# Converting the weights in 32 pieces among the attention's steps instead of 16 calls between them

## The chip, the core and the metric

The kernel runs on one core of one Trainium2 chip. The metric is the device time of one execution in microseconds (us). The core's engines are TensorE (PE: matrix products and transposes, with PEld for its weight loads), VectorE (DVE), ScalarE (ACT), GpSimd (POOL) and SyncE (SP), which issues most DMA transfers. Each engine works through its own queue of instructions in order, and semaphores tie the queues together.

## What is computed

Two blocks follow one another. The first is attention in which a query sees only keys of its own cluster; the second is a feed-forward block (ffn) with an unusual gate.

```
B, H, S, D = 4, 8, 768, 64;  16 clusters
q_assign = argmax(q_n . c_n), k_assign = argmax(k_n . c_n)      # normalised
scores   = q k^T / sqrt(D), -1e9 where q_assign != k_assign
attn     = softmax(scores);  y = attn v                         # (B, H, S, D)
x        = y as (B*S, H*D) = (3072, 512)
h        = x w_in                                               # w_in  512 x 2048
g        = h * erf(softplus(h))
out      = g w_out                                              # w_out 2048 x 512
```

The weights w_in and w_out arrive as 64-bit floats, of which the kernel sees pairs of 32-bit words (low word, high word). It makes 32-bit floats of them by integer and float operations on the words: a shift of the high word, a mask that turns numbers too small into zero, the low word scaled by the number's power of two and added, and the sign put back. Everything else is 32-bit float, with some tiles in bf16.

## The kernel before

**Attention.** The 32 pairs (batch, head) are worked off two heads at a time, as 16 "pairs" p; four of them (HP) make a batch. For each pair `route(p)` (L212) transposes q and k on TensorE (tile `pt`), ScalarE copies them out of PSUM (L228, L230), and GpSimd casts them to bf16 into the lower half of `qm` and `km` (L232). Then come the similarities to the centroids (`psim`, `sims`), their maxima on VectorE (`mx` L257, L259, `mr` L267 with GpSimd's product L263 between them), the one-hot codes `aq` and `ak` (L269), and their transposes `pb` (L282), copied into `qm` and `km` (L290, L292). `shift(p)` (L297) makes 12 tiles `sm` of masked maxima and reduces each on VectorE (`nmx`, L308); the result `nm` (L313) goes through DRAM (`line`, L322 and L325) into one row of `qm`.

`scores(u)` (L338) works on one of a pair's 12 units (half of the queries, one of NJ = 6 key blocks): four products into `sc` (L345, L351), ScalarE's exponential into `pr` (L356) and GpSimd's running sum `acc` (L360, L364). `attend(u0)` (L368) makes the products with v for a half (`av`, L375) and the sums (`psum`, L382); VectorE adds a constant (L386), takes the reciprocal (L387) and writes the ffn's input `xT` in three chunks (L396).

**The ffn.** There are 12 chunks of 256 tokens, three to a batch. `hidden(n)` (L424) makes `hp` (L432), copied to `g` (L439); `gate(n)` (L408) runs softplus and erf on ScalarE over the tile `a_s` in two halves each (L415) and multiplies on VectorE (L417); `project(n)` (L446) makes `po` (L451), `osb` and the output transfer.

**The order.** The program issues `route(0)` and `shift(0)`, then two units at a time. After each two units come five slots; in each slot `pump` (L482) issues ffn products up to an allowance of TensorE cycles (`per_slot`) and one step of the next pair's `route` and `shift` (`aside`, L492) is issued. A batch's ffn starts when its four pairs have been attended, so the first four pairs run without ffn, and the last batch's ffn stands alone at the end. The framework's scheduler then orders the instructions of each engine by the order of issue and by when their data and buffers are ready in its own plan; the order on an engine is fixed before the run.

**The conversion.** `convert` (L130) is called 16 times, for 128 x 1024 weights each: after two of every three double units of the first four pairs. Each call loads 1 MB into `raw64` through GpSimd's queue (L132), squares the high words on ScalarE (L138), and has seven operations on VectorE (L139, L144, L148, L151, L154, L157, L158) on the tiles `w_m` and `w_x`. The pools for raw words and scratch are closed when the fourth pair is nearly done, and the pools for `a_s`, `g` and `osb` are opened in their place (L515 to L519).

Of the kernel before, what the change touches and what calls it, by code (L numbers as in the profile page):

```python
# [17 lines left out]
P = 128  # L18
# [9 lines left out]
GW = 2  # L28
TB = 256
NCHUNK = B * S // TB  # L30
LC = 1024
TINY_HI = 2.0**-15 * 1.125
BIG = 2.0**60
# [4 lines left out]
XBUFS = (5, 6, 6)  # L38
# [4 lines left out]
def kernel(  # L43
# [22 lines left out]
    xTp = pool("xTp", 1)  # L66
    linep = pool("linep", 2, space=bass.MemoryType.DRAM)
# [37 lines left out]
    wpool = ExitStack()  # L105
    setup = wpool.enter_context(tc.tile_pool(name="setup", bufs=1))
# [20 lines left out]
    wraw = wpool.enter_context(tc.tile_pool(name="wraw", bufs=2))  # L127
    wtmp = wpool.enter_context(tc.tile_pool(name="wtmp", bufs=2))

    def convert(dst, src):  # L130
        raw = wraw.tile([P, LC, 2], U32, name="raw64")
        nc.gpsimd.dma_start(out=raw.rearrange("p (a n) w -> p a (n w)", a=src.shape[1]), in_=src)  # L132
        hi, lo = raw[:, :, 1], raw[:, :, 0]
        m = wtmp.tile([P, LC], U32, name="w_m")
        x = wtmp.tile([P, LC], U32, name="w_x")
        mf, xf = m.bitcast(F32), x.bitcast(F32)

        nc.scalar.activation(out=xf, in_=raw.bitcast(F32)[:, :, 1], func=ACT.Square)  # L138
        nc.vector.tensor_scalar(  # L139
            out=x.bitcast(I32), in0=xf, scalar1=TINY_HI**2, scalar2=-1.0,  # L140
            op0=ALU.is_ge, op1=ALU.mult,
        )

        nc.vector.tensor_scalar(  # L144
            out=m, in0=hi, scalar1=3, scalar2=0x7FFFFFFF,
            op0=ALU.logical_shift_left, op1=ALU.bitwise_and,
        )
        nc.vector.scalar_tensor_tensor(  # L148
            out=m, in0=m, scalar=0x40000000, in1=x, op0=ALU.bitwise_xor, op1=ALU.bitwise_and
        )  # L150
        nc.vector.tensor_scalar(  # L151
            out=x, in0=m, scalar1=0x7F800000, scalar2=None, op0=ALU.bitwise_and
        )
        nc.vector.scalar_tensor_tensor(  # L154
            out=xf, in0=lo, scalar=2.0**-52, in1=xf, op0=ALU.mult, op1=ALU.mult
        )
        nc.vector.tensor_tensor(out=xf, in0=mf, in1=xf, op=ALU.add)  # L157
        nc.vector.scalar_tensor_tensor(  # L158
            out=dst.bitcast(U32), in0=hi, scalar=0x80000000, in1=x,
            op0=ALU.bitwise_and, op1=ALU.bitwise_or,  # L160
        )

    w_steps = []
    for c in range(0, DFF, LC):
        for r in range(DM // P):
            rows = moe_w_in[r * P : (r + 1) * P, 2 * c : 2 * (c + LC)]
            w_steps.append((w_in[:, r, c : c + LC], rows.unsqueeze(1)))
    n = LC // DM
    for f in range(0, NFT, n):
        rows = moe_w_out[f * P : (f + n) * P].rearrange("(t p) m -> p t m", p=P)  # L170
        w_steps.append((w_out[:, f : f + n].rearrange("p t m -> p (t m)"), rows))
# [3 lines left out]
    sq = setup.tile([P, D], F32, name="sq")  # L175
# [20 lines left out]
    cn = setup.tile([P, 2, D], F32, name="cn")  # L196
# [15 lines left out]
    def route(p):  # L212
        st = pairs[p]
        for nm in "qk":
# [3 lines left out]
            for half in range(2):  # L218
# [6 lines left out]
                dst = raw[:, half * HW : (half + 1) * HW]  # L225
                src = pt.rearrange("p j t -> p (j t)")
                if nm == "q":
                    nc.scalar.mul(out=dst, in_=src, mul=D**-0.5)  # L228
                else:
                    nc.scalar.copy(out=dst, in_=src)  # L230
                for e in range(2):
                    nc.gpsimd.tensor_copy(  # L232
                        out=low[(1 - e) * D : (2 - e) * D, e, half * HW : (half + 1) * HW],
                        in_=raw[e * D : (e + 1) * D, half * HW : (half + 1) * HW],
                    )
# [32 lines left out]
        for i, (dst, op) in enumerate(((aq, ALU.is_equal), (ak, ALU.not_equal))):  # L268
# [7 lines left out]
            )  # L276
        yield
# [90 lines left out]
    def attend(u0):  # L368
# [17 lines left out]
        nc.vector.tensor_scalar_add(out=den, in0=psum, scalar1=S * EPS)  # L386
# [21 lines left out]
    def gate(n):  # L408

        h = gs[n]  # L410
        s = late_pools["act"].tile([P, NFT, TB], F32, name="a_s")
        half = NFT // 2
        for func, src in ((ACT.Softplus, h), (ACT.Erf, s)):
            for i in range(0, NFT, half):
                nc.scalar.activation(out=s[:, i : i + half], in_=src[:, i : i + half], func=func)  # L415
        for i in range(0, NFT, GW):
            nc.vector.tensor_tensor(  # L417
                out=h[:, i : i + GW], in0=s[:, i : i + GW], in1=h[:, i : i + GW], op=ALU.mult
            )

    gs = {}
    late_pools = {}

    def hidden(n):  # L424
        b, c = n // CPB, n % CPB
        gs[n] = late_pools["g"].tile([P, NFT, TB], F32, name="g")
        for fp in range(NFT // GW):
            hp = ps_f.tile([P, GW, TB], F32, name="hp", tag="f")
# [17 lines left out]
    def project(n):  # L446
        b, c = n // CPB, n % CPB
        for tt in range(TJ):
            po = ps_f.tile([P, DM], F32, name="po", tag="f")
            for ft in range(NFT):  # L450
                nc.tensor.matmul(  # L451
# [5 lines left out]
            osb = late_pools["out"].tile([P, DM], F32, name="osb")  # L457
# [5 lines left out]
    def ffn_stream():  # L463

        late = iter(())
        for n in range(NCHUNK):
            while (n // CPB + 1) * HP > len(xTs):
                yield None
            for i, cost in enumerate(hidden(n)):
                yield cost  # L470
                if i >= 2 * GW * HP:
                    for _ in range(2):
                        if (x := next(late, None)) is not None:
                            yield x
# [83 lines left out]
```

## Time and profile before

| | |
|---|---|
| median of 3 runs | 1337.95 us (1336.57 to 1338.3) |
| the profiled execution, its own time | 1337.45 us |
| its span, first to last instruction | 1335.5 us |
| PE busy | 1218.0 us (91%) |
| DVE busy | 640.5 us (48%) |
| ACT busy | 421.0 us (32%) |
| POOL busy | 400.2 us (30%) |
| mean granted TensorE clock | 0.966 |

The busy time of an engine is the time in which at least one of its instructions ran; the time in which it only waited or set registers is not counted. In the rows of a group, "x16 | 27.5, 1718 | 0.3" means 16 instructions, 27.5 us busy together, 1718 ns the mean of one, and 0.3 us in which the engine stood idle just before them. In a timeline row the first number is the start in us, the second the length in us, and square brackets tell how long the engine had been idle and what released it. In a table of stretches each row is one part of the span; the columns are the length, each engine's busy time with its instructions in brackets, the granted TensorE clock, the share in which the DMA engines were busy, and the rate. A row of waits has the total, how often, and the longest, in us.

### The profile page before, as it was taken

The numbers are of one execution on the slowest core, as the hardware profiler recorded it, in microseconds if no ns is written. First come the engines' busy times: TensorE is split into PE (matmuls) and PEld (weight loads), VectorE is DVE, ScalarE is ACT, GpSimd is POOL, SyncE is SP. The second block draws the span as 40 slices with busy tenths as digits, with TensorE's granted clock in tenths as the row PEclk, the third lists the DMA queues.
The fourth block names the chain that finished last, engine by engine and source line by source line (L and its number), as shares of the span: only waits on it lengthen the run. The fifth ranks groups of instructions, "written<-read, shape, count | busy, mean of one in ns | idle before, by whom it ended". The sixth has DMA issues, their size and how long they took to land.

```text
span 1335.5 us, 13090 instructions
## 1 busy us (share of the span) xinstructions
PE 1218.0 (91%) x5313; PEld 659.5 (49%) x5313; DVE 640.5 (48%) x809; ACT 421.0 (32%) x458; POOL 400.2 (30%) x337
## 2 busy tenths in 40 slices
PE   3676767889999999999999999999999999999998
PEld 1222222346546545444654645545645646575764
DVE  6898999746243525451634534452615413221221
ACT  3232323224416224414423422514424413130321
POOL 3536365452323233423233231522232221000000
PEclk9777889899999999999999999999999999999999
DMA  6213142110101001101001010102000000000000
GB/s 166 87 64 120 42 130 75 24 37 1 36 8 32 12 13 40 36 1 40 12 1 51 2 44 8 36 1 52 1 9 20 1 8 9 8 9 8 8 16 16
DMA packets 82699, 42.90 MB, mean 32 GB/s; under 512 B 76464, under 2 KB 76496, under 8 KB 81616
## 3 DMA queue, kind: packets, MB, share of 16 engines
q1 hardware_dynamic: 79312, 25.31, 7.7%
q0 software_dynamic: 3328, 16.78, 3.7%
q8 instruction: 41, 0.67, 0.2%
q14 instruction: 18, 0.15, 0.0%
HBM read 35.73 MB, written 6.34 MB: 32 GB/s over the span
## 4 chain that ended last, share of the span: by engine, by line
PE 72%; DVE 16%; POOL 4%; ACT 3%; DMA 2%; issue 2%; SPq 0%; POOLq 0%; ACTq 0%; DVEq 0%
PE po L451 24%; PE hp L432 21%; PE av L375 8%; PE sc L345 7%; PE sm L304 4%; DVE nmx L308 3%; DVE den L387 2%; POOL acc L364 2%; PE psum L382 2%; ACT pr L356 2%; PE sc L351 2%; DVE w_x L154 2%; PE pt L221 1%; DVE w_x L157 1%; DVE w_m L148 1%
## 5 line engine op out<-in xcount | busy, mean ns | idle before, releaser
L432 PE MATMUL hp<-xT,w_in 128*128 128x256 f32 x1536 | 379.6, 384 | 0.0
L451 PE MATMUL po<-w_out,g 128*128 128x512 f32 x768 | 370.4, 599 | 2.6 <-DVE g L439 2.0
L364 POOL TENSOR_TENSOR acc<-acc,pr 128x768 f32<-128x768 f32 x128 | 224.2, 1751 | 489.8 <-ACT pr L356 483.0
L432 PEld LDWEIGHTS hp<-xT,w_in 128*128 128x128 f32 x1536 | 284.8, 191 | 99.2 <-issue 67.0
L356 ACT ACTIVATE pr<-sc 128x768 f32<-128x768 f32 x192 | 152.5, 812 | 386.7 <-PE sc L351 384.5
L308 DVE TENSOR_REDUCE nmx<-sm 128x2 f32<-128x768 f32 x192 | 178.6, 953 | 110.0 <-PE sm L304 108.7
L439 DVE COPY g<-hp 128x512 f32<-128x512 f32 x96 | 66.0, 688 | 286.8 <-PE hp L432 286.6
L345 PE MATMUL sc<-qT,kT 64*128 64x384 f32 x768 | 187.1, 549 | 10.3 <-DVE nmx L308 8.4
L451 PEld LDWEIGHTS po<-w_out,g 128*128 128x128 f32 x768 | 139.4, 190 | 107.4 <-issue 90.6
L375 PE MATMUL av<-pr,in_v 128*64 128x386 f32 x768 | 160.1, 511 | 6.6 <-DVE xT L396 6.2
L304 PE MATMUL sm<-km,qm 128*128 128x384 bf16 x384 | 99.1, 347 | 25.8 <-DVE nmx L308 13.7
L345 PEld LDWEIGHTS sc<-qT,kT 64*128 64x128 f32 x768 | 69.2, 199 | 92.5 <-issue 42.1
L360 POOL TENSOR_TENSOR acc<-pr,pr 128x768 f32<-128x768 f32 x32 | 60.6, 1894 | 152.8 <-ACT pr L356 152.6
L375 PEld LDWEIGHTS av<-pr,in_v 128*64 128x64 f32 x768 | 54.8, 139 | 85.4 <-issue 74.8
L415 ACT ACT_TABLE_LOAD x48 | 61.6, 1283 | 105.3 <-DVE g L439 104.5
L417 DVE TENSOR_TENSOR g<-a_s,g 128x512 f32<-128x512 f32 x96 | 66.2, 740 | 50.5 <-ACT a_s L415 50.5
L386 DVE TENSOR_SCALAR den<-psum 128x384 f32<-128x384 f32 x32 | 17.8, 556 | 147.9 <-PE psum L382 147.7
L304 PEld LDWEIGHTS <-qm 128*128 128x128 bf16 x384 | 36.3, 100 | 98.7 <-issue 84.2
L387 DVE RECIPROCAL den<-den 128x384 f32<-128x384 f32 x32 | 81.6, 2550 | 0.7
L351 PE MATMUL sc<-qm,km 64*128 64x384 bf16 x384 | 70.8, 339 | 0.2 <-DMA qm<-line 0.2
L415 ACT ACTIVATE a_s<-g 128x2048 f32<-128x2048 f32 x24 | 45.9, 1911 | 78.4 <-DVE g L439 78.3
L292 ACT COPY km<-pb 64x768 bf16<-64x768 bf16 x32 | 25.4, 793 | 117.8 <-PE pb L282 117.4
(76 smaller groups left out, 720.9 us busy)
## 6 DMA issues: line engine op xcount, KB each, us to landing
raw<-in_moe_w_in_dram POOLq DMA_DIRECT2D x8, 1024.0 KB, 5.7
raw<-in_moe_w_out_dram POOLq DMA_DIRECT2D x8, 1024.0 KB, 5.3
in_q<-in_q_dram SPq DMA_DIRECT2D x32, 192.0 KB
in_k<-in_k_dram SPq DMA_DIRECT2D x32, 192.0 KB
in_v<-in_v_dram SPq DMA_DIRECT2D x32, 192.0 KB
out_dram<-osb SPq DMA_DIRECT2D x24, 256.0 KB
qm<-line SPq DMA_DIRECT2D x32, 1.5 KB
line<-nmT SPq DMA_DIRECT2D x16, 3.0 KB
```

Of the source, the lines that this page charges most:

```text
L304: nc.tensor.matmul(sm[:, e, 0:HW], lhsT=st["qm"][:, e, t * P : (t + 1) * P], rhs=st["km"][:, e, half * HW : (half + 1) * HW], start=True, ...
L308: nc.vector.tensor_reduce(out=nmx[:, t, half], in_=sm[:, :, 0:HW], axis=AX.X, op=ALU.max, negate=True)
L345: nc.tensor.matmul(sc[:, e, 0:HW], lhsT=st["kT"][r, j * P : (j + 1) * P], rhs=st["qT"][r, cols], start=True, stop=False,)
L351: nc.tensor.matmul(sc[:, e, 0:HW], lhsT=st["km"][r, e, j * P : (j + 1) * P], rhs=st["qm"][r, e, cols], start=False, stop=True,)
L356: nc.scalar.activation(out=pr[:, :, 0:HW], in_=sc[:, :, 0:HW], func=ACT.Exp)
L364: nc.gpsimd.tensor_tensor(out=st["acc", half], in0=st["acc", half], in1=pr[:, :, 0:HW], op=ALU.add)
L375: nc.tensor.matmul(av[e * D : (e + 1) * D], lhsT=st["v"][:, j, e], rhs=prs[(u0 + j) % NPT][:, e], start=(j == 0), stop=(j == NJ - 1),)
L387: nc.vector.reciprocal(out=den, in_=den)
L415: nc.scalar.activation(out=s[:, i : i + half], in_=src[:, i : i + half], func=func)
L417: nc.vector.tensor_tensor(out=h[:, i : i + GW], in0=s[:, i : i + GW], in1=h[:, i : i + GW], op=ALU.mult)
L432: nc.tensor.matmul(hp[:, a], lhsT=w_in[:, r, f0 : f0 + P], rhs=xTs[b * HP + r][c], start=(r == 0), stop=(r == HP - 1),)
L451: nc.tensor.matmul(po, lhsT=gs[n][:, ft, tt * P : (tt + 1) * P], rhs=w_out[:, ft], start=(ft == 0), stop=(ft == NFT - 1),)
```

## The change

The conversion becomes a generator of three steps a piece, on 128 x 512 weights, 32 pieces. `prepare` draws steps from it: 1.5 for each step of `aside(0)`, 0.4 a slot in the first four pairs, and one a slot after that. The mask is made by ScalarE's Sign in place of L139, the addition L157 goes to GpSimd, and the raw words and the scratch lie in halves of the gate's tile `a_s`, which is now two buffers of half the size. Raw words are loaded through SP's queue, one piece ahead. All pools are open from the start; `hidden` and `project` are held back while the weights they need aren't issued. In `route`, ScalarE writes the bf16 copies directly from PSUM (three reads of each `pt`), and there is one more empty step ahead of `pb`. In `attend`, ScalarE adds the constant. `attend` for a finished half is issued right after the next half's first two units instead of ahead of the second two. `pump` keeps what it owes, up to 8 slots' worth, and issues at most twice the allowance at once. The second of the three xT chunks has 5 buffers instead of 6.

```diff
-LC = 1024
+LC = 512
+TINY_SQ = TINY_HI**2 * (1 - 2.0**-23)
-XBUFS = (5, 6, 6)
+XBUFS = (5, 5, 6)
...
+    actp = pool("actp", 2)
+    gp = pool("gp", 2)
+    outp = pool("outp", 2)
+    setup = pool("setup", 1)
...
+    def half_tile():
+        return actp.tile([P, NFT // 2, TB], F32, name="a_s")
+
+    def convert():
+        def fetch(n):
+            t = half_tile().rearrange("p f t -> p (f t)").bitcast(U32)
+            nc.sync.dma_start(out=t[:, 0 : 2 * LC], in_=w_steps[n][1])
+            raw = t[:, 0 : 2 * LC].rearrange("p (n w) -> p n w", w=2)
+            return raw, t[:, 2 * LC : 3 * LC], t[:, 3 * LC : 4 * LC]
+
+        def finish(n, raw, x):
+            nc.vector.scalar_tensor_tensor(
+                out=w_steps[n][0].bitcast(U32), in0=raw[:, :, 1], scalar=0x80000000, in1=x,
+                op0=ALU.bitwise_and, op1=ALU.bitwise_or,
+            )
+            converted[0] = n + 1
+
+        nxt, last = fetch(0), None
+        for n in range(len(w_steps)):
+            raw, m, x = nxt
+            hi, lo = raw[:, :, 1], raw[:, :, 0]
+            mf, xf = m.bitcast(F32), x.bitcast(F32)
+            nc.scalar.activation(out=xf, in_=hi.bitcast(F32), func=ACT.Square)
+            nc.scalar.activation(out=x.bitcast(I32), in_=xf, func=ACT.Sign, scale=-1.0, bias=tiny)
+            nc.vector.tensor_scalar(
+                out=m, in0=hi, scalar1=3, scalar2=0x7FFFFFFF,
+                op0=ALU.logical_shift_left, op1=ALU.bitwise_and,
+            )
+            if last:
+                finish(*last)
+            if n + 1 < len(w_steps):
+                nxt = fetch(n + 1)
+            yield
+            nc.vector.scalar_tensor_tensor(
+                out=m, in0=m, scalar=0x40000000, in1=x, op0=ALU.bitwise_xor, op1=ALU.bitwise_and
+            )
+            yield
+            nc.vector.tensor_scalar(
+                out=x, in0=m, scalar1=0x7F800000, scalar2=None, op0=ALU.bitwise_and
+            )
+            nc.vector.scalar_tensor_tensor(
+                out=xf, in0=lo, scalar=2.0**-52, in1=xf, op0=ALU.mult, op1=ALU.mult
+            )
+            nc.gpsimd.tensor_tensor(out=xf, in0=mf, in1=xf, op=ALU.add)
+            last = n, raw, x
+            yield
+        finish(*last)
...
-                dst = raw[:, half * HW : (half + 1) * HW]
-                if nm == "q":
-                    nc.scalar.mul(out=dst, in_=src, mul=D**-0.5)
-                else:
-                    nc.scalar.copy(out=dst, in_=src)
-                for e in range(2):
-                    nc.gpsimd.tensor_copy(
-                        out=low[(1 - e) * D : (2 - e) * D, e, half * HW : (half + 1) * HW],
-                        in_=raw[e * D : (e + 1) * D, half * HW : (half + 1) * HW],
-                    )
+                own = [(slice(e * D, (e + 1) * D), low[(1 - e) * D : (2 - e) * D, e, cols]) for e in range(2)]
+                for r, dst in [(slice(0, P), raw[:, cols])] + own:
+                    if nm == "q":
+                        nc.scalar.mul(out=dst, in_=src[r], mul=D**-0.5)
+                    else:
+                        nc.scalar.copy(out=dst, in_=src[r])
...
+        yield
         yield
...
-        nc.vector.tensor_scalar_add(out=den, in0=psum, scalar1=S * EPS)
+        nc.scalar.activation(out=den, in_=psum, func=ACT.Identity, bias=alleps)
...
+            while converted[0] < DM // P * ((fp + 1) * GW * P // LC):
+                yield None
...
+                while converted[0] < DM // P * (DFF // LC) + ft + 1:
+                    yield None
...
     def pump(cycles):
         owed[0] += cycles
-        while owed[0] > 0:
+        left = 2 * cycles
+        while owed[0] > 0 and left > 0:
             cost = next(stream, None)
             if cost is None:
-                owed[0] = 0
-                return
+                break
             owed[0] -= cost
+            left -= cost
+        owed[0] = min(owed[0], 8 * cycles)
...
+    def prepare(tenths):
+        due[0] += tenths
+        while due[0] >= 10:
+            due[0] -= 10
+            next(conv, None)
+
     for _ in aside(0):
-        pass
+        prepare(15)
...
-        if j == 2 and u >= NJ:
-            attend(u - 2 - NJ)
         scores(u)
         scores(u + 1)
-        if p < HP and j != 2 and w_steps:
-            convert(*w_steps.pop(0))
-        if (p, half, j) == (HP - 1, 1, NJ - 2):
-            wpool.close()
-            late_pools.update(act=pool("actp", 1), g=pool("gp", 2), out=pool("outp", 2))
+        if j == 0 and u:
+            attend(u - NJ)
         for _ in range(SLOTS):
-            pump(per_slot)
+            if len(xTs) >= HP:
+                pump(per_slot)
+            prepare(4 if p < HP else 10)
             next(ahead, None)
```

In the new file the piece's instructions stand at L167 (Square), L168 (Sign), L169, L178, L183, L186 (VectorE), L189 (GpSimd's addition) and L155 (`finish`).

## The prediction

> **What bounds the kernel now.** I read the page's slices first, then a table of busy time by stretch, then the groups of one line by shape, then VectorE (DVE) in order of time.
>
> ```profile
> span 1335.5 us, 13090 instructions
> PE   3676767889999999999999999999999999999998
> DVE  6898999746243525451634534452615413221221
> PEclk9777889899999999999999999999999999999999
> ```
>
> From the ninth slice TensorE is at 9 tenths and at full clock: there the time is TensorE's work. In the first eight slices (33.4 us each) TensorE stands at 3 to 8 and DVE at 9. I cut the span where each `shift` ends (the one row of `nm`, L313: 40.75, 93.7, 158.9, 217.4, 274.0):
>
> ```profile
> core 0: us, PE busy (x) PEld busy (x) DVE busy (x) ACT busy (x) POOL busy (x), PEclk, DMA share, GB/s
> 0.00:40.75 40.75, 19.40 (x66) 8.07 (x68) 28.45 (x65) 10.07 (x13) 10.34 (x29) 1.00 0.52 136
> 40.75:93.70 52.95, 33.93 (x138) 12.29 (x136) 48.26 (x50) 15.01 (x20) 24.10 (x19) 0.69 0.30 95
> 93.70:158.90 65.20, 43.80 (x194) 16.51 (x192) 59.73 (x59) 17.81 (x24) 31.67 (x23) 0.84 0.26 83
> 158.90:217.40 58.50, 44.05 (x196) 16.44 (x194) 55.97 (x57) 17.81 (x24) 33.57 (x23) 0.88 0.32 92
> 217.40:274.00 56.60, 41.95 (x198) 16.22 (x196) 47.33 (x47) 14.68 (x21) 30.12 (x20) 0.89 0.14 40
> ```
>
> Four pairs of heads take 53 to 65 us each and DVE is busy for 84 to 96% of that. After 274.0 TensorE is busy 1034.90 of 1061.50 us. So the change can win only in the first 274 us, in TensorE's 26.6 idle us after them, or by putting TensorE's later work earlier. What fills DVE there is the conversion, 16 calls of seven operations:
>
> ```profile
> L154 DVE SCALAR_TENSOR_TENSOR w_x<-raw,w_x 128x1024 f32<-128x1024 uint32 x16 | 27.5, 1718 | 0.3
> L157 DVE TENSOR_TENSOR w_x<-w_m,w_x 128x1024 f32<-128x1024 f32 x16 | 25.0, 1560 | 0.2
> L148 DVE SCALAR_TENSOR_TENSOR w_m<-w_m,w_x 128x1024 uint32<-128x1024 uint32 x16 | 23.9, 1491 | 0.3
> L151 DVE TENSOR_SCALAR w_x<-w_m 128x1024 uint32<-128x1024 uint32 x16 | 16.8, 1048 | 0.3
> L139 DVE TENSOR_SCALAR w_x<-w_x 128x1024 int32<-128x1024 f32 x16 | 14.8, 927 | 8.5 <-ACT w_x L138 8.4
> L144 DVE TENSOR_SCALAR w_m<-raw 128x1024 uint32<-128x1024 uint32 x16 | 14.4, 898 | 6.3 <-DMA raw<-in_moe_w_in_dram 6.3
> ```
>
> With L158 (24.6 us) that is 147 of the 240 us that DVE is busy before 274. The means are above the shortest instances (1.21 us for the four operations with two inputs or two steps on them, 0.68 for the three plain ones): 16 x (4 x 1.21 + 3 x 0.68) = 110, so 37 us are stretch. In time it looks so:
>
> ```profile
> 94.93 0.69 DVE L139 TENSOR_SCALAR w_x<-w_x 128x1024 int32<-128x1024 f32 x1
> 95.54 2.17 DVE L151 TENSOR_SCALAR w_x<-w_m 128x1024 uint32<-128x1024 uint32 x1
> 97.63 2.17 DVE L144 TENSOR_SCALAR w_m<-raw 128x1024 uint32<-128x1024 uint32 x1
> 99.72 2.70 DVE L154 SCALAR_TENSOR_TENSOR w_x<-raw,w_x 128x1024 f32<-128x1024 uint32 x1
> ```
>
> While POOL runs `acc` additions without a gap (three in 6.10 us from 95.24), every such DVE operation takes 1.48 us more, the 0.69 one as the 1.21 one.
>
> **The change on DVE.** Seven operations on 1024 elements become five on 512, 32 times. From the shapes of L396 (0.48 us for 256, 0.34 for 128: 1.06 ns an element) a 512 form costs 1.21 - 0.54 = 0.67, and the plain form at half that slope 0.41. A piece: 3 x 0.67 + 2 x 0.41 = 2.8; 32 pieces 91 us. The stretch is not known. Low: POOL's casts go as well (42.9 us of its work) and its instructions are no more than before, so a little under the 37 stays, 34, and DVE needs 125 (3.9 a piece). High: only POOL's long operations cause it, 41 `acc` and 5 products with `rank`, 0.8 us each, and the 32 new additions do the same: 37 + 26 = 63, so 154 (4.8 a piece). I take 3.9, because in 274 us POOL's busy time hardly changes: 129.8 - 42.9 + 32 x 1.2 (1.68 us for 768 elements in L364, with a fixed part) = 125. Both ends stay for the range.
>
> The Trainium skill, "SBUF — State Buffer", section "Who interferes with whom", speaks against small pieces: DVE with two inputs in SBUF, or in its two-port mode, and a GpSimd operation that reads SBUF exclude one another for a whole instruction. The 2.17 beside 0.69 agrees. By that rule the loss is per meeting, not per element, and the sum would be nearer to 154 than to 125.
>
> DVE busy before the fifth `shift` ends: 240 - 147 - 7 x 0.55 (L386 goes to ScalarE) + 125 = 214 us. It was idle 34. That alone would put the end at 248; but the new order adds waits, so I go by stretch. The built program's order on each engine shows that all 32 pieces stand on DVE ahead of the fifth `route`, none beside the ffn: 7 before the first `nm`, then about 7, 8, 8 and 2.
>
> **The waits it adds.** Square waits for its load on ScalarE; behind it stand exps, and TensorE's scores wait for those (ScalarE already idles 58.7 us at L138 for loads, and TensorE at most 4.2 us for ScalarE's exps there). L155 waits on DVE for POOL's addition, which may stand behind an `acc`; behind it stand reductions that free the score banks. The order puts the next piece's L169 or a reduction between, so from nothing to 32 x 1.2 = 38 us; nearest is `mr` waiting for POOL's product, 2.9 us in all: I take 0.2 us a piece, within the stretches below.
>
> **Start to first `nm`, 40.75 now: 57.** On ScalarE, Square and Sign of piece 0 stand before the first copy of `qT` (now at 7.34). They wait for a load queued on SP behind q and k; the first raw tile now lands at 10.36, so `qT` comes at about 11.5: +4. Each transposed half is now read by ScalarE three times (0.49 + 2 x 0.48); half of that hides behind `in_k`, for which TensorE waits 2.49 us now: +2. Two pieces stand before the first `mx`: the first `nmx` at 34 instead of 28.6. Between the twelve `nmx` (11.06 us without gaps now) stand four pieces, 11.6 us: 34 + 23 = 57.
>
> **Second stretch, 53 now: 50.** `nm` to `mx` 16: the mask line's way through DRAM (6 us from `nm` to L351, as at 274.0 to 280.1), then ScalarE in order: two exps, low copies, Square and Sign of two pieces, `sims`. `mx` to `nmx` 11 (9.3 now where nothing else is there, 246.60 to 255.92, and two pieces in its gaps). `nmx` to `nm`: twelve reductions 11.4, reciprocal and `xT` 3.3, two pieces 8: 23.
>
> **Third and fourth, 65.2 and 58.5 now: 55 each.** The order gives TensorE, between `nm` and `psim`, 10 score products (0.46), 11 mask products (0.17), 15 `av` (0.43), transposes and sums (3.7): 16.6 us at full clock, 20 at the 0.84 to 0.88 granted here, and 2 to `mx`: 22. Then 11 and 22. DVE's sum is 8 x 3.9 + 21.2 = 52, just below. **Fifth, 56.6 now: 49**: 22, 9.3 and 18 (255.92 to 273.96), as the rows of this stretch without conversion.
>
> 57 + 50 + 55 + 55 + 49 = 266: 8 us earlier than 274.
>
> **After that.** The remaining 1061.5 us are TensorE's. By the built order one score, five `av` and three hidden products fewer are left at the fifth `nm`: 0.5 + 2.1 + 1.5 = -4. Between halves of a transpose TensorE has some 1.4 us of other work, ScalarE needs 1.45: half of 33 gaps lose 0.25 us, +4 (without this cover of three hidden products it would be 1 us a gap, +33). 10 of the 26.6 idle us lie at 504 to 556, 634 to 660 and 920 to 946, where the next batch's attention runs with little ffn; the order gives these pairs about twice the ffn products (the pairs ahead of them fewer): -4. The wait of L282 for `aq` stays (same products ahead of it):
>
> ```profile
> PE pb L282 <- DVE aq L269: 13.3, 10, 2.4
> ```
>
> XBUFS of 5 holds one `av` back until a chunk's hidden products are done; TensorE has those meanwhile: 0. `gate` by halves does the same four activations: 0. ScalarE gets some 5 us a pair (345.6 busy of 1061.5): off the path. No table load stands at Square, Sign or Identity in the order. SP gets 32 loads of 512 KB between q, k and line transfers; a piece asks two ahead, 4 us (1 MB lands in 5.5), inside the 6 to 7 us of a piece.
>
> Sum: 1335.5 - 8 - 4 = 1323.5; the profiled run was 1337.45 for that span (+1.95), and the median of the runs 1337.95, 0.5 above it. **Forecast 1325 us**, own range 1315 to 1333.
>
> **Rivals.**
> - *DVE's sum is the bound* (chance 0.22). For: DVE is 84 to 96% busy now. Against: the chain `nm` to `mx`. The fifth `nm` at 248: 26 + 4 earlier, 1307.
> - *The order eats it* (0.14): pieces at the start cost 16 to 18 us, the pairs give back just as much (52 + 57 + 57 + 51 after 58): 275, 1334 to 1337. For: TensorE's 22 us ahead of `mx` in every pair. That the change does not do what it says belongs here: nothing is left beside the ffn.
> - *The shared port makes it slower* (0.25). The 32 additions and 160 shorter operations meet POOL more often: 4.8 us a piece, 154 - 125 = 29 us on a path that DVE sets: 1354. It decides from 4.3 us a piece (12 us of gain over 32 pieces). For: 2.17 for 0.69. Against: the casts go.
>
> Forecast 0.39. The range 1302 to 1352 takes in both ends of the stretch and leaves out under 2 in 10. Faster by over 0.2% (2.7 us, about what a measurement can tell): the forecast, the first rival and a part of the second, 0.64; within 0.2%: 0.10; slower: 0.26.
>
> **What would show it.** The first `nm` at 57 and the fifth at 266; the rows of the five operations at 0.7 to 1.0 and 0.5 to 0.7 us mean; POOL's addition at 1.2; TensorE's busy time unchanged near 1218; no table load before 290 us but the first two. A first `nm` past 65, pieces above 4.3 us or TensorE idle more than 35 us after the fifth `nm` would make it wrong.

## The result, and the profile after

The changed kernel takes **1399.3 us** (median of 4 runs, 1396.21 to 1399.7), the kernel before 1337.3 (1335.77 to 1338.3): ratio **1.046** [1.0441, 1.0479], 61 to 62 us slower, where 1325 was forecast in a range up to 1352. The profiled execution took 1399.7 us for a span of 1397.9.

The slices of the page of after:

```profile
span 1397.9 us, 13314 instructions
PE   2566666779999999999999999999999999999998
DVE  5777777643625343525343342525342342221211
PEclk9987777889999999999999999999999999999999
```

TensorE stands at 9 from the tenth slice in both, but a slice is 34.9 us here and 33.4 before, and between the first slice and the tenth TensorE stands at 5 to 7 where it stood at 6 to 8. VectorE, which mostly stood at 8 or 9 in the first stage, stands at 7: it has become emptier, and the stage longer. The table by stretch, cut at the `nm` rows as before (length, busy us of each engine, granted clock, DMA share, GB/s):

```profile
core 0: us, PE busy (x) PEld busy (x) DVE busy (x) ACT busy (x) POOL busy (x), PEclk, DMA share, GB/s
0.00:54.78 54.78, 19.29 (x65) 7.97 (x66) 40.19 (x93) 21.26 (x34) 12.33 (x25) 1.00 0.48 129
54.78:120.47 65.69, 43.99 (x163) 15.27 (x162) 44.88 (x61) 25.59 (x41) 26.08 (x17) 0.85 0.24 69
120.47:191.93 71.46, 47.94 (x192) 17.88 (x192) 53.40 (x68) 28.92 (x46) 29.60 (x19) 0.76 0.26 76
191.93:263.57 71.64, 48.14 (x192) 17.91 (x192) 53.48 (x68) 29.00 (x46) 29.62 (x19) 0.76 0.26 76
263.57:317.24 53.67, 43.67 (x190) 16.94 (x191) 26.01 (x32) 19.94 (x32) 17.45 (x11) 0.83 0.10 23
317.24:1397.90 1080.66, 1050.86 (x4513) 583.56 (x4511) 387.15 (x512) 408.81 (x473) 221.93 (x135) 1.00 0.07 18
```

The first stage ends at 317.2 instead of 274.0 (+43.2), and what follows lasts 1080.7 instead of 1061.5 (+19.2). In the first stage no engine is full: in the third stretch VectorE is busy 53.4 of 71.5 us (59.7 of 65.2 before), TensorE 47.9, at a granted clock of 0.76 (0.84 before). Over the whole first stage TensorE is idle 23 us longer than before (114.2 against 90.9) and busy 20 us longer (203.0 against 183.1). So the time went partly into waits of one engine for another and partly into longer work of TensorE. In the part that TensorE sets, TensorE is *busy* 16 us longer (1050.9 against 1034.9) and idle only 3 us longer (29.8 against 26.6).

VectorE's longest waits up to 330 us (total, times, longest):

```profile
DVE nmx L327 <- PE sm L323: 30.0, 32, 4.3
DVE a_s L178 <- ACT a_s L168: 18.8, 9, 3.1
DVE w_in L155 <- POOL a_s L189: 13.4, 9, 2.9
DVE w_out L155 <- POOL a_s L189: 11.8, 10, 1.4
DVE mx L275 <- PE pt L270: 10.7, 2, 7.7
DVE den L406 <- ACT den L405: 10.2, 2, 8.5
```

44 us are waits for the two operations that were taken off VectorE (Sign L168, the addition L189); 41 are waits for TensorE; 10 are waits for the constant that ScalarE now adds (L405). On TensorE, waits over the whole span:

```profile
PE pb L301 <- DVE aq L287: 25.5, 10, 5.7
PE pt L242 <- ACT qm L251: 22.9, 20, 4.5
PE pn L337 <- DVE nm L332: 22.6, 6, 6.1
PE hp L454 <- DVE xT L415: 12.0, 5, 3.0
...
PE psim L260 <- ACT km L253: 7.3, 8, 1.5
...
PE pt L242 <- ACT km L253: 1.8, 2, 1.5
```

The rows of `pt` and `psim` have TensorE waiting for ScalarE's bf16 copies, the second and third read of a transposed half: 32.0 us in 30 waits. Before, the same products waited for ScalarE's one read, 24.3 us in 10 waits:

```profile
PE pt L221 <- ACT qT L228: 12.9, 5, 6.7
PE psim L242 <- ACT kT L230: 10.3, 3, 9.1
...
PE pt L221 <- ACT kT L230: 1.1, 2, 0.6
```

So the waits for ScalarE are not new; they have become many short ones instead of a few long ones, and 7.7 us more in sum. What has no row before is the third line, TensorE's wait for `nm` with the transpose `pn`, 22.6 us. It is 22.6 in run 13 and 19.9 in run 4 as well, 4.4 in run 2 without the arithmetic, and absent in run 11: it comes with the conversion in the new order, and no run undid it alone.

### The profile page after: what moved, and what is told of

Read it like the earlier page. It is cut to its first block, busy times and chain, and to the rows that moved or that the text cites. A ratio compares the mean times of both kernels' runs of the same rounds, so it can differ in the third digit from the quotient of the medians.

```text
span 1397.9 us, 13314 instructions
## 1 busy us (share of the span) xinstructions
PE 1253.9 (90%) x5313; PEld 659.5 (47%) x5313; DVE 605.1 (43%) x827; ACT 533.5 (38%) x672; POOL 337.0 (24%) x225
## 4 chain that ended last, share of the span: by engine, by line
PE 68%; ACT 7%; DVE 5%; issue 2%; POOL 2%; POOLq 0%; ACTq 0%; DVEq 0%
PE po L475 23%; PE hp L454 19%; PE sc L364 8%; PE av L394 8%; PE sm L323 4%; PE sc L370 2%; PE psum L401 1%; PE pt L242 1%; DVE nmx L327 1%; POOL acc L383 1%; ACT pr L375 1%; DVE den L406 1%; ACT qm L251 1%; ACT a_s L435 1%; PE pb L301 1%
## 5 line engine op out<-in xcount | busy, mean ns | idle before, releaser
L383 POOL TENSOR_TENSOR acc<-acc,pr 128x768 f32<-128x768 f32 x128 | 218.4, 1706 | 522.6 <-ACT pr L375 512.0
L364 PE MATMUL sc<-qT,kT 64*128 64x384 f32 x768 | 205.0, 560 | 9.0 <-ACT pr L375 4.1
L394 PE MATMUL av<-pr,in_v 128*64 128x386 f32 x768 | 170.4, 514 | 4.9 <-DVE xT L415 4.9
L323 PE MATMUL sm<-km,qm 128*128 128x384 bf16 x384 | 104.5, 352 | 16.7 <-DVE nmx L327 11.4
L364 PEld LDWEIGHTS sc<-qT,kT 64*128 64x128 f32 x768 | 74.4, 199 | 94.3 <-issue 50.4
L394 PEld LDWEIGHTS av<-pr,in_v 128*64 128x64 f32 x768 | 55.2, 139 | 88.1 <-issue 80.4
L437 DVE TENSOR_TENSOR g<-a_s,g 128x512 f32<-128x512 f32 x96 | 61.8, 701 | 47.7 <-ACT a_s L435 47.4
L370 PE MATMUL sc<-qm,km 64*128 64x384 bf16 x384 | 76.8, 342 | 0.0
L189 POOL TENSOR_TENSOR a_s<-a_s 128x512 f32<-128x512 f32 x32 | 41.6, 1302 | 105.2 <-DVE a_s L186 86.9
L405 ACT ACTIVATE den<-psum,alleps 128x384 f32<-128x384 f32 x32 | 18.6, 581 | 113.5 <-PE psum L401 81.0
```

Source lines behind the costliest of these rows:

```text
L323: nc.tensor.matmul(sm[:, e, 0:HW], lhsT=st["qm"][:, e, t * P : (t + 1) * P], rhs=st["km"][:, e, half * HW : (half + 1) * HW], start=True, ...
L364: nc.tensor.matmul(sc[:, e, 0:HW], lhsT=st["kT"][r, j * P : (j + 1) * P], rhs=st["qT"][r, cols], start=True, stop=False,)
L370: nc.tensor.matmul(sc[:, e, 0:HW], lhsT=st["km"][r, e, j * P : (j + 1) * P], rhs=st["qm"][r, e, cols], start=False, stop=True,)
L383: nc.gpsimd.tensor_tensor(out=st["acc", half], in0=st["acc", half], in1=pr[:, :, 0:HW], op=ALU.add)
L394: nc.tensor.matmul(av[e * D : (e + 1) * D], lhsT=st["v"][:, j, e], rhs=prs[(u0 + j) % NPT][:, e], start=(j == 0), stop=(j == NJ - 1),)
L437: nc.vector.tensor_tensor(out=h[:, i : i + GW], in0=s[i // half][:, i % half : i % half + GW], in1=h[:, i : i + GW], op=ALU.mult,)
```

## The experiments

Two theories after these profiles. **H**: the hand-overs of each piece (VectorE waits for Sign and for GpSimd's addition) cost the time. **S**: ScalarE's three reads of each transposed half cost it. To keep the conversion's arithmetic apart from the rest, some kernels only load the weights. Runs without an interval are a single execution each; the kernel before took 1337.2 to 1339.1 beside them. Single executions of the kernel before lie between 1335.4 and 1340.3, so a difference of 3 us between two such runs can be chance.

**1, 2. Both kernels without the conversion's arithmetic.** Diff: the operations from Square to the last `or` go, and each load writes rows of q into the weight tile.

> The kernel before with the conversion's arithmetic left out: each call only loads 512 KB of other floats (from q) straight into the weight tile, so the output is not the reference's. It shows the first stage without conversion. All theories: pairs of 47 us, as the row of the fifth stretch without conversion said (22 + 9.3 + 18, minus a little), fifth nm near 226, so about 1288 us (1337 - 49). If it stays above 1320, the conversion was not what the first stage waited for.

> The changed kernel with the conversion's arithmetic left out in the same way (32 loads of 256 KB from q, output not the reference's). Theory H, hand-overs: the loss of the first stage (43 us) comes from the conversion's waits on VectorE for ScalarE's Sign (18.8 us) and GpSimd's addition (25.2 us), so without it the new kernel's first stage equals that of the run before it, and only the 19 us of the ffn stage remain: 1300 to 1310. Theory S, ScalarE's three reads of each transposed half (TensorE waits 17.6 us for them in the first stage): it keeps its loss, about 1335 to 1345.

Measured: before 1282.7, after 1328.1. So 45.5 of the 61 us are there when nothing is converted: 26.4 by the fifth `nm` (245.8 against 219.4), 19 after it. The arithmetic itself costs 55.5 us before and 71.2 after, 15.7 more. H can at most be a part.

**3, 4. One part undone in the changed kernel.**

```diff
# e3
-            nc.scalar.activation(out=x.bitcast(I32), in_=xf, func=ACT.Sign, scale=-1.0, bias=tiny)
+            nc.vector.tensor_scalar(out=x.bitcast(I32), in0=xf, scalar1=TINY_HI**2, scalar2=-1.0, ...)
-            nc.gpsimd.tensor_tensor(out=xf, in0=mf, in1=xf, op=ALU.add)
+            nc.vector.tensor_tensor(out=xf, in0=mf, in1=xf, op=ALU.add)
# e4: ScalarE copies pt into the row tile only; GpSimd makes the bf16 copies from the row tile
```

> The changed kernel with Sign back on VectorE as a comparison and the addition back on VectorE: same arithmetic, same 32 pieces, seven operations on VectorE. VectorE gets 32 x (0.42 + 0.69) = 36 us more work. Theory H: the 44 us of waits go and more than that work is given back, 1370 to 1390. Theory S: the work is added to the path, 1410 to 1435.

> The changed kernel with the bf16 copies back on GpSimd, from the float copy in SBUF. Theory H: no change in the first stage, 1390 to 1405, a few us less where TensorE waited for ScalarE in the ffn stage. Theory S: 25 to 45 us less, 1355 to 1375.

Measured: 1389.3 (-10.0) and 1373.0 (-26.3). Run 3 takes the 44 us of waits away and puts 34 us of busy time on VectorE in the first stage (251.9 against 218.3), so its 10 us are the net of both, and not the price of the waits. GpSimd's copies give 10.6 us back by the fifth `nm` (306.6) and 16.2 after it (of 26.8 by the spans), where the kernel is TensorE's.

**5, 6. The same without arithmetic.** Load-only as run 2, with the bf16 copies on GpSimd; then also the product with v back at j = 2.

> The changed kernel with its pieces only loaded, not converted (the seven operations on each piece are left out and the weights are rows of q), and with the bf16 copies of q and k back on GpSimd, made from the transposed rows in SBUF. The same kernel with the copies on ScalarE took 1328.1 us, and the kernel before without conversion 1282.7. Theory S (ScalarE's three reads of each transposed half hold PSUM's one transpose buffer longer, whatever the conversion does): undoing them gains what it gained beside the conversion, 26 us, so 1302. Rival C (the copies cost only because ScalarE also has Square and Sign in its queue): without the conversion at most 10 of the 26 are there, so 1318 to 1328. With S some 20 us of the 45 are still to be found.

> As the run above (pieces only loaded, copies back on GpSimd), and the product of a half with v put back where it stood before: ahead of the scores of j = 2, two steps after the half's last scores, and not behind the scores of j = 0. Theory O (in its new place the product stands on TensorE behind scores that have just been issued and waits for the last Exp and GpSimd's last addition, with all hidden products behind it): the 20 us still missing go, so 1283 to 1290. Rival (the missing time is in the pump, the extra step ahead of the gate's matrices or the reciprocal's input on ScalarE): no more than 5 us less than the run above, so 1297 to 1302.

Measured: 1292.1 (-36.0) and 1295.2 (+3.0). S holds, and more strongly than expected: the copies alone are 36 of the 45.5 us. TensorE's waits for ScalarE at `pt` and `psim` fall from 22.2 to 4.5 us with them. The product's new place costs nothing that can be told from chance; theory O falls.

**7. Three edits undone, converting** (copies on GpSimd, seven operations on VectorE, product at j = 2).

> The changed kernel, converting, with three edits undone at once: bf16 copies on GpSimd, Sign and the addition on VectorE, product with v at j = 2. If the gains add up (26 for the copies, 10 for the seven operations, and whatever the run above gains by the product's place), 1399 - 36 = 1363 less that gain; under theory O 1343 to 1350, under its rival 1358 to 1363. If copies and additions meet on GpSimd or VectorE again, it ends above 1366.

Measured: 1365.5. The gains add up (1399.3 - 26.3 - 10.0 + 3 = 1366); 28 us over the kernel before were still to be placed.

**8. The copies alone, in the kernel before.** Diff: the three ScalarE reads of the change in `route`.

> The kernel before with one edit of the change alone: the bf16 copies of q and k made by ScalarE from PSUM. Theory S: 26 us as in the changed kernel, so 1364. Rival C (the copies cost only beside Square and Sign in the new order, or only with the product with v in its new place): within 8 of the kernel before, 1330 to 1346; below it if GpSimd's copies cost VectorE more by the port than ScalarE's reads cost the chain.

Measured: 1352.7, 15 us slower: between the two. The cost is there in the old order too, a little over half as large; 10.5 of the 15 by the fifth `nm` (284.5 against 274.0).

**9, 10. The conversion of w_out beside the ffn, in the kernel before.** Diff: scratch in tiles of `g` and in half tiles of the gate, 1024 columns kept, all seven operations as before.

```diff
...
-        if p < HP and j != 2 and w_steps:
-            convert(*w_steps.pop(0))
+        if w_steps and (j == 0 if p < HP else True):        # e10: j == 0 and (p < 2 or half)
+            convert(*w_steps.pop(0), p >= HP)
```

> The kernel before, with one idea of the change kept: the conversion needs no buffers of its own. Its 16 batches of 1024 columns keep their seven operations on ScalarE's Square and VectorE and their size; the scratch is a tile of g in the first stage and two half tiles of the gate afterwards. The eight batches of w_in stay behind the scores of j = 0 of the first four pairs, two for each pair where four were; the eight of w_out move to the fifth and sixth pair, beside the hidden products. Theory P (what a batch costs depends on the stage: some 3.1 us in the four stretches of the first stage, from 233 us with 16 batches against 183 us without, and under 0.5 us beside the ffn, where TensorE has products to put in): 1338 less eight times 2.6 to 3.1, 1313 to 1318. Rival (beside the ffn a batch costs as much, since its 9 us on VectorE hold back the reductions that the shift waits for): 1333 to 1343.

> As the run above, with two of the eight batches of w_in moved as well: six in the first stage, and ten beside the ffn, one for each step of the fifth pair and the first four of the sixth. Theory P: another 5 to 6 us less, 1307 to 1313, if VectorE's 9 us a batch still fit beside the reductions. Rival: hidden products now wait for their weights or the shift for VectorE, and it is no faster than the run above or slower.

Measured: 1348.7, ratio 1.0076 [1.0057, 1.0096], and 1351.8, ratio 1.0113 [1.0084, 1.0142]. Both are about 1% slower, with intervals clear of 1, and the gain of 20 to 31 us that theory P forecast is not there. The fifth `nm` came at 264.8 instead of 274.0 in run 9, but one later stretch (314.9 to 403.0) took 88.1 us where it took 73.3, with TensorE idle 8.4 of them. Five of the eight batches of w_out stood ahead of 290 us on VectorE anyway, put there by the scheduler, so only three really moved. Both kernels also lack the sixth buffer of the second `xT` chunk, which run 15 prices at 8.7, and have the gate's tile in halves. So these runs do not show what a batch beside the ffn costs by itself.

**11. Three more edits undone, load-only**: one step less ahead of `pb`, the constant added on VectorE, the old account of owed products.

> The changed kernel with its pieces only loaded, not converted (the seven operations are left out and the weights are rows of q), bf16 copies on GpSimd, product with v at j = 2 (these took 1295.2 us), and three more edits undone: no extra step ahead of the gate's matrices, the sum's constant added on VectorE, and the kernel before's way to keep account of owed products. Kernel before without conversion: 1282.7. If one of these three holds what is left of the skeleton, 1283 to 1287; if not, 1291 to 1297, and what is left lies with the loads on SP's queue and the tiles they use, or with one buffer less for xT.

Measured: 1288.6 (-6.5). The fifth `nm` stands at 219.4, as in the kernel before without conversion; what was left lay after it.

**12. Halves, in the kernel before.** Diff: each operation of a batch twice on 512 columns.

> The kernel before with each operation of a batch issued twice on 512 columns, instead of once on 1024; loads, places and engines unchanged. The traces have 0.69 us for 512 columns where 1024 took 1.22, so VectorE gets 16 x 7 x 0.16 = 18 us more. If that lies open as the rest of the conversion does (50 of 147 us), 6 us more, 1344; if all of it does, 1356; if halves give the reductions a place to slip in between, 1335 or less.

Measured: 1340.1 (+2.8), less than expected, although the seven operations took 177 us where they took 147. Small pieces as such are cheap. The run says less about VectorE's sum: some of its operations slid behind the fifth `nm`, and others overlap their neighbours, so that up to there VectorE is busy 247.2 us where it was 239.8, and the fifth `nm` is 2.5 us later. A third of what was added lies open, as the expectation had it. The stretches of this run: between 38.6 and 276.5 VectorE is busy 220 of 238 us, TensorE at a clock of 0.85.

```profile
38.60:276.50 237.90, 170.91 (x716) 62.48 (x716) 219.93 (x305) 66.56 (x102) 107.15 (x85) 0.85 0.26 76
```

**13. What about the copies costs.** Same engine, same number, other source:

```diff
-                for r, dst in [(slice(0, P), raw[:, cols])] + own:
-                    ... copy(out=dst, in_=src[r])              # src = pt, in PSUM
+                ... copy(out=raw[:, cols], in_=src)
+                for r, dst in own:
+                    nc.scalar.copy(out=dst, in_=raw[r, cols])  # the row tile, in SBUF
```

> The changed kernel with ScalarE's bf16 copies reading the row tile in SBUF that ScalarE has just written, and not PSUM; same engine, same count, one read of PSUM's transpose buffer instead of three. If the cost of the copies (26 us against GpSimd) is that the one transpose buffer is held while three reads pass, most of it goes: 1375 to 1385. If it is that the copies stand in ScalarE's queue ahead of what TensorE and VectorE wait for, nothing goes: 1394 to 1402.

Measured: **1376.6 (-22.7)**. ScalarE is as busy as it was (533.5 us in both), so its time is not what costs: how long the one `pt` bank is held is. From the start of a half's first transpose to the end of ScalarE's last read of it the traces have a median of 1.07 us before, 2.07 in after and 1.27 in run 13. (The pool of `pt` has one buffer, which `psim`, `pb`, `pn` and `psum` share.) Timeline of ScalarE and TensorE in after, third stretch (start, length, in brackets idle before and releaser):

```profile
133.45 0.67 ACT L167 ACTIVATE a_s<-a_s 128x512 f32<-128x512 f32 x1 [3.23 <-DMA a_s<-in_moe_w_out_dram]
134.02 0.47 ACT L251 ACTIVATE qT<-pt 128x384 f32<-128x384 f32 x1
134.50 0.98 ACT L251 ACTIVATE qm<-pt 64x384 bf16<-64x384 f32 x2
```
```profile
135.54 0.90 PE L242 MATMUL pt<-ident,in_q 128*128 128x128 f32 x3 [3.71 <-ACT qm L251]
```

and of ScalarE in run 13, where the two copies read SBUF:

```profile
131.55 0.47 ACT L250 ACTIVATE qT<-pt 128x384 f32<-128x384 f32 x1
131.92 0.80 ACT L376 ACTIVATE pr<-sc 128x768 f32<-128x768 f32 x1
132.75 1.03 ACT L254 CAST qm<-qT 64x384 bf16<-64x384 f32 x2
```

In after, the next three transposes start when the third read ends, and all that was issued to TensorE later stands behind them. ScalarE itself had waited 3.23 us for a piece's load ahead of the first read, so a late load holds the bank too. In run 13 the same waits of TensorE are shorter, since the bank is free after one read (18.2 us in sum, where after had 32.0):

```profile
PE pt L242 <- ACT qT L250: 12.6, 7, 3.9
...
PE pt L242 <- ACT kT L252: 4.6, 6, 1.3
...
PE psim L261 <- ACT kT L252: 1.0, 3, 0.6
```

The last stretch of run 13 is 1066.8 instead of 1080.7, 13.9 of the 22.7 us. Of these, 8.6 are TensorE's busy time (1042.3 against 1050.9) and 5.3 its idle time:

```profile
308.01:1374.80 1066.79, 1042.29 (x4513) 581.43 (x4511) 386.76 (x512) 408.75 (x473) 221.83 (x135) 1.00 0.07 18
```

So the shorter hold did not act by waits alone. The scheduler planned with it and built another order: 649 of TensorE's 5313 products stand in another place than in after. The 22.7 us are both together.

**14. No pieces ahead of the first `nm`.** Diff: `prepare(15)` in the loop over `aside(0)` becomes `pass`.

> The changed kernel with no steps of the conversion drawn while the first pair is prepared; the pieces so left over are drawn in the fifth pair, one step a slot, beside hidden products. The first stretch, 54.8 us, was 38.9 with pieces loaded but not converted, so some 7 pieces lie open there for 16 us. If a piece costs what it costs anywhere in the first stage and little beside the hidden products, 1399 - 16 + 11 x 0.5 = 1385 to 1390. If pieces beside hidden products cost as much as at the start (8 batches moved there in an earlier run gained nothing), 1396 to 1404.

Measured: 1387.2 (-12.1), as expected in sum, but in other parts. First and last stretch:

```profile
0.00:42.57 42.57, 18.97 (x64) 7.81 (x65) 26.53 (x70) 15.85 (x26) 7.50 (x21) 1.00 0.39 106
...
287.98:1385.40 1097.42, 1057.91 (x4513) 585.43 (x4511) 414.06 (x552) 417.25 (x488) 232.62 (x143) 0.99 0.08 21
```

The first stage ends 29 us earlier (288.0), the rest takes 17 us longer: pieces moved beside the hidden products are cheaper than at the start, and not nearly free.

**15. The buffer of xT**, load-only: run 11 with `XBUFS = (5, 6, 6)`.

> As the run of the changed kernel that has its pieces only loaded (seven operations left out, weights are rows of q), copies on GpSimd, product at j = 2 and three more edits undone (1288.6 us), with six buffers for the second xT chunk again instead of five; room for it comes from opening the output pool where the setup tiles were. If the missing buffer holds the last 6 us, 1282 to 1284, as the kernel before without conversion (1282.7); if not, 1287 to 1290, and the half-size gate tiles are left.

Measured: 1279.9 (-8.7). The missing buffer holds the rest of the skeleton's loss, and with it back the new skeleton is 2.8 us below the old one, which can be chance. The stretches after the fifth `nm` (219.4 in run 11, 217.0 here) take 1067.4 and 1060.8:

```profile
219.40:1286.80 1067.40, 1043.70 (x4539) 591.54 (x4535) 399.96 (x538) 342.37 (x354) 269.23 (x223) 1.00 0.07 18
```
```profile
217.00:1277.80 1060.80, 1034.92 (x4538) 590.72 (x4535) 401.01 (x538) 345.55 (x356) 270.36 (x223) 1.00 0.07 18
```

The buffer's price is busy time of TensorE, 8.8 us, and no wait: TensorE is idle 23.7 us there with five buffers and 25.9 with six.

**16, 17, 18. What can be kept.** Diff of 16 and 17: `nc.gpsimd.dma_start` becomes `nc.sync.dma_start` for the raw words, in the kernel before. 18 also makes the mask by Sign on ScalarE, on 1024 columns.

> The kernel before with the raw words loaded through SP's queue, as in the change, and nothing else. The first shift ends at 35.1 us with loads on SP and at 36.3 with loads on GpSimd's queue where nothing is converted, and GpSimd loses 16 issues of 0.7 to 1.1 us: 1330 to 1336 if GpSimd's issues or the early loads cost something; 1340 to 1350 if loads on SP stand in the way of the mask line's three transfers, for which the scores wait.

> The kernel before with the raw words loaded through SP's queue, again, now with an interval. One look had it 4.9 us below the kernel before on the same chip. If the first stretches gain 2.7 us by the first shift and the rest lasts as long, the ratio is 0.996 to 0.998; if the one look was chance, 0.999 to 1.001.

> The run above, with the mask made by ScalarE's Sign in place of VectorE's is_ge, on 1024 columns. VectorE loses 16 operations, 14.8 us busy; at the share that lies open (50 of 147 us) 5 us less, 1328 to 1330. If VectorE waits for Sign as it did in the changed kernel (18.8 us for 32 pieces), it gives that back: 1334 to 1344.

Measured: 1334.2 in a single execution; then 1334.4, ratio 0.9976 [0.9967, 0.9986]; with Sign 1331.95, ratio **0.9959** [0.9941, 0.9976], a little less gain than expected. Run 18 is 0.4% faster than the kernel before, a small gain but clear of 1. VectorE waits for Sign 2.8 us there in the first 290, against 18.8 in the changed kernel. The gain of run 17 does not lie where it was expected: its first `nm` comes at 42.2, later than the 40.75 of the kernel before, and its fifth at 272.0 instead of 274.0.

**The ledger**, in us:

| part | load-only runs | converting, undone alone |
|---|---|---|
| ScalarE's bf16 copies from PSUM | 36.0 (run 2 to 5) | 26.3 (on GpSimd), 22.7 (from SBUF) |
| product with v at j = 0 | -3.0 (5 to 6) | |
| extra step, constant, account of owed products | 6.5 (6 to 11) | |
| one xT buffer fewer | 8.7 (11 to 15) | |
| all else in the skeleton | -2.8 (15 against 1) | |
| arithmetic: Sign and addition, net | | 10.0 (run 3) |
| arithmetic: pieces at the start | | 12.1 (run 14) |

The left column sums to the 45.4 us of the skeleton, from single executions; its two negative rows can be chance. The arithmetic adds 15.7; runs 3 and 14 each undo a part of that, and their sum of 22 shows that the two overlap each other or the skeleton's waits. How they share it was not taken apart.

## Why the prediction was wrong, by its steps

- **What bounds the kernel**: right as read (the first stage VectorE's, the rest TensorE's), but I looked for an effect only in the first 274 us, in TensorE's idle time and in work moved ahead. 16 of the 62 us are longer busy time of TensorE after that. They lie in the attention's products: from the fifth `nm` on, the busy time with `sc` rose by 9.0 us, `sm` by 2.9, `psum` by 2.2, `av` by 1.3 and `pt` by 0.9, and that of the ffn's `hp` and `po` in sum not at all. Two undoings are together of this size: the copies' source (run 13, 8.6 us less) and the `xT` buffer (run 11 to 15, 8.8 less). Both change the order that the scheduler builds. What such an order can cost shows in the rows: two heads' products on halves of the array run side by side. Before, at 600 us, four records of `sc` (two heads) take 0.92:

```profile
600.11 0.92 PE L345 MATMUL sc<-qT,kT 64*128 64x384 f32 x4
600.86 0.33 PE L351 MATMUL sc<-qm,km 64*128 64x384 bf16 x2
```

and in after two records (one head), with other work put between the heads, take as long:

```profile
329.69 0.91 PE L364 MATMUL sc<-qT,kT 64*128 64x384 f32 x2
330.53 0.55 PE L242 MATMUL pt<-ident,in_k 128*128 128x128 f32 x3
...
331.44 0.59 PE L364 MATMUL sc<-qT,kT 64*128 64x384 f32 x1
331.45 0.33 PE L370 MATMUL sc<-qm,km 64*128 64x384 bf16 x1
```

  Counted in the traces after the fifth `nm`, the records of `sc`, `av` and `psum` that start with no other of their kind within 0.06 us are 134 before, 192 in after, 138 in run 13, 170 in run 11 and 132 in run 15. So both undoings bring the partners together again. Run 13's TensorE is nevertheless busy 7.4 us longer there than before, so the parting is not all of it; no run changed it alone.
- **VectorE's sum**: predicted 125 us, measured 126.9 (26.7 + 22.7 + 21.6 + 20.5 + 35.4 for L178, L186, L183, L169, L155). Right. The Trainium skill, "SBUF — State Buffer", section "Who interferes with whom", was given as the reason for the 154 end: shorter operations would meet GpSimd more often. The stretch over the shortest lengths was 37 us for 112 operations on 1024 columns before, 36 for 160 on 512 in after, and 52 for 224 on 512 in run 12: 0.33, 0.22 and 0.23 us an operation. So a short operation loses less than a long one, and the loss is neither one price for each operation nor one for each element.
- **Start to first `nm`, 57**: measured 54.8. Right. What was missing is that these pieces gave nothing back: run 14 ends the first stage 29 us earlier without them, 17 of which come back later.
- **The waits it adds, 0.2 us a piece, at most 38 in all**: VectorE's waits for Sign and the addition are 18.8 + 25.2 = 44 us, 1.4 a piece, above even the upper bound. Too low; undoing them, for 34 us more work on VectorE, gained 10.
- **The step that failed: ScalarE's three reads of each transposed half**, priced at +2 at the start and +4 in the rest, and in the stretches between with no wait of TensorE. Runs 13 and 4 price them at 22.7 to 26.3 us, of which 13.9 to 16.2 in the rest, and runs 2 and 5 at 36.0 without the arithmetic. In the stretches I added up TensorE's products and VectorE's pieces at their lengths, and gave TensorE no wait for ScalarE between the transposes, though it has just one bank for them. For the rest, the +4 was nearer than the +33 that I gave for lost cover, but it counted waits alone: 8.6 of run 13's 13.9 us are busy time, from the other order that the scheduler builds when the bank is held longer.
- **The stretches of 50, 55, 55 and 49**, which this step feeds: measured 65.7, 71.5, 71.6 and 53.7. In the third: `nm` to `mx` 28.3 (predicted 22), `mx` to first `nmx` 10.3 (11), `nmx` to `nm` 32.9 (22). The reads explain a part of these 51 us only. The arithmetic, which was to become cheaper, costs 71.2 us where it cost 55.5; how much of that is the 22.6 us of TensorE's wait for `nm` stays open.
- **"XBUFS of 5 ... 0"**: wrong, 8.7 without conversion, a term that was put at nothing. TensorE does have hidden products in that time, and still needs longer, since it is busy 8.8 us longer.
- **Idle over 35 us after the fifth `nm` would make it wrong**: it is 29.8. The first `nm` and the pieces stayed within their limits too. So none of the signs against the forecast came up, as much of the loss went into busy time: TensorE's is 1253.9, where 1218 was forecast, and the fifth `nm` stands at 317 instead of 266.
- **No table load** for Sign, Square and Identity in the first stage, addition 1.2 us: right (none; 1.30).
- **Rivals**: "DVE's sum is the bound" does not hold for the changed kernel: up to the fifth `nm` VectorE is busy 218.0 us instead of 239.8, and the `nm` comes 43 us later. "The order eats it" was right that the pieces at the start are not given back, but its 275 for the fifth `nm` lies far from 317. "The shared port makes it slower" had the right sign and the wrong mechanism: a piece costs 126.9 / 32 = 3.97 us, below the 4.3 from which it was to decide.
- **Small errors in the working**: 1323.5 + 1.95 + 0.5 is 1326, not 1325. In the slices DVE stands at 6 to 9 ahead of the ninth, and TensorE reaches 9 in the tenth. The casts' 42.9 us and the 41 `acc` are counts up to 290 us; up to 274 they are 38.9 and 36. None of these explains the miss.

## What to carry to other kernels

A tile with one buffer belongs to the engine that reads it until its last read: moving a copy from "SBUF on an idle engine" to "PSUM on another" lengthens the hold, and the bill comes on the engine that writes the tile next, here TensorE, on which everything stands in one queue. When an engine is nearly full in a stage, check that emptying it shortens the stage: halving the operations kept VectorE busy 7.4 us longer in the first stage for 2.5 us of time, and the change made it 21.8 us less busy and lost 43. A buffer given up for room, and an order that parts products which ran side by side, are terms of the sum too; both can show as busy time with no wait.

## What the runs showed of the hardware that was not expected

- ScalarE's two bf16 copies of 64x384 take 0.98 us from PSUM and 1.03 from SBUF; the slower source made the kernel 22.7 us faster, with the bank held 1.27 us instead of 2.07 (medians).
- One head's score product alone takes 0.91 us, two heads' together 0.92.
- The granted clock is 1.00 in the first stretch, with TensorE busy 19.3 of 54.8 us, and 0.76 in the third and fourth, with 48 of 71.5; without conversion it is 0.91 in the same stage (run 15), with 152.3 of 181.8. No rule by the share of busy time comes out of these rows: the second stretch was granted 0.69 before with TensorE busy 33.9 of 53.0 us, and 0.85 in after with 44.0 of 65.7. Nor does the granted clock alone set the length of a product: `sm` takes a median of 0.50 us in the first stretch, 0.34 in the third and 0.33 after the fifth `nm`, where the clock is 1.00 again.
- VectorE's operations on 512 columns, run in the old places, took 20% more in sum than those on 1024 for the same words (177 against 147 us).
